# A fused retention and gated-convolution kernel: spreading the first batch over three engines, using spare PSUM banks for chunk 1, masks behind scores, value products between chunks

## Chip, cores, metric

One core of a Trainium2 chip (trn2). The metric is the device time of one execution in microseconds (us). A traced span is 1.7 to 2.2 us shorter than the time of the same run. The experiments ran on four chips, one for each group of kernels, together with the kernel before. Times of kernels in different groups are compared by their ratios to the kernel before, or by many runs together; single traces are also compared across groups. A run over 1.5% above the fastest of the same kernel counts as slow; ratios and means of "fast runs" leave it out.

## The reference

Retention (linear attention with a decay per head) feeds a gated unit: a causal depthwise convolution of five taps makes the gate, a matmul the value, their product goes through an output matmul.

```python
q, k, v: (8, 8, 576, 64) float32      # batch, heads, sequence, head size
scores = (q @ k.T) / sqrt(64)
ret    = scores * Dmat                # Dmat[i, j] = gamma_h ** (i - j) for i >= j, else 0
x      = (ret @ v) as (8, 576, 512)
gate   = sigmoid(sum_k conv_w[k] * x shifted by 4 - k)      # five taps
out    = (gate * (x @ w_val)) @ w_out                       # float32
```

## The kernel before

A sequence of 576 is cut into four chunks of 128 and a tail of 64, whose two halves of a pair of batches share a chunk: 36 chunks. A chunk runs these steps: keys turned on TensorE (`turn_k`), `scores`, `masks` on VectorE, the part from earlier chunks (`carried`), `values`, `take_x` (eviction with decay on VectorE), `update` of the state and `take_state` on ScalarE. Two chunks make a unit: `conv`, `gate` on ScalarE, two halves of `value` with a product z on VectorE, two halves of `project`. Engines run their own instruction streams in program order, so the order of the Python calls is the schedule. `keep_warm` issues matmuls whose result nobody reads. In this text DVE is VectorE, ACT ScalarE, POOL GpSimd, SP SyncE.

```python
ps_t  = ... bufs=1    # turned tiles "tps"          PSUM pools: 1 + 2 + 1 + 1 + 3 banks
ps_s  = ... bufs=1    # "s0", "s1": scores
ps_o  = ... bufs=1    # "o": output of a chunk
ps_st = ... bufs=1    # state
ps_g  = ... bufs=3    # "g": gates, values, projections, keep_warm

def load_keys(t):                     # float32 to bf16 during the transfer, GpSimd's queue
    kb = bfp.tile([P, H, D], BF16, name="kb", bufs=LA + 3)
    nc.gpsimd.dma_start(out=kb, in_=k[...])
def cast_k(t):                        # only chunk 0: loaded as float32 through SP's queue
    nc.vector.tensor_copy(kb, loaded["k", *chunks[t]])
def cast_v(t):
    nc.gpsimd.tensor_tensor(vb, loaded["v", ...], gin[...], op=ALU.mult)
def scores(t):
    s = [ps_s.tile([P, NP, P], F32, name=f"s{i}") for i in range(2)]
    ...
def carried(t):
    o = ps_o.tile([P, NP, P], F32, name="o")
    ...
# start of the program (cut: constants, diagonals, loads)
keep_warm(9)
for r in range(RQ):
    cast_q(("batch", 0, r), nc.vector if r % 2 else nc.gpsimd)
for r in range(RQ):
    turn_q(("batch", 0, r), s_copy if r % 2 else v_copy, ps_g if r < 3 else None)
cast_v(0); load_keys(2)
scores(0); turn_k(1); masks(0, 0); masks(0, 1); carried(0); update(0); take_state(0)
scores(1); values(0); cast_v(1); load_keys(3); take_x(0)
masks(1, 0); masks(1, 1); carried(1); update(1); take_state(1); values(1); take_x(1)
# ...
conv(0); gate(0, 0); gate(0, 1); load_wo()
turn_k(2); carried(2); scores(2); value(0, 0); masks(2, 0); cast_v(2); masks(2, 1); value(0, 1)
for t in sbl: nc.vector.memset(t, 0.0)
values(2); take_x(2); update(2); take_state(2)
turn_k(3); carried(3); scores(3); masks(3, 0); masks(3, 1); load_keys(4)
keep_warm(4); project(0, 0); project(0, 1); keep_warm(4)
cast_v(3); values(3); take_x(3); update(3); take_state(3); load_keys(5)
conv(1); gate(1, 0); gate(1, 1)
# ... cast_q of batch 1, cast_v(4), turn_k(4)
value(1, 0); turn_q(("batch", 1, 0)); value(1, 1)
# ... the other three turn_q, turn_k(5)
carried(4); update(4); scores(4); masks(4, 0); masks(4, 1)
for t in range(4, NT + 2):            # the loop; not touched but for where unit 1 starts
    ...
```

Of the kernel before, what the change touches and what calls it, by code (L numbers as in the profile page):

```python
# [21 lines left out]
def kernel(  # L22
# [48 lines left out]
    with tc.manual_schedule():  # L71
# [41 lines left out]
        load_one("k", k, *chunks[0], 1)  # L113
        load_queries(0)
        load(0)
# [40 lines left out]
        load_keys(1)  # L156
# [56 lines left out]
        def cast_k(t):  # L213
            kb = bfp.tile([P, H, D], BF16, name="kb", bufs=LA + 3)
            nc.vector.tensor_copy(kb, loaded["k", *chunks[t]])  # L215
            kbf[t] = kb

        def cast_v(t):
            vb = bfp.tile([P, H, D], BF16, name="vb")
            nc.gpsimd.tensor_tensor(vb, loaded["v", *chunks[t]],  # L220
                                    gin[:, chunks[t][2], :].unsqueeze(2).to_broadcast([P, H, D]), op=ALU.mult)
            vbf[t] = vb
# [4 lines left out]
        def cast_q(job, eng=nc.gpsimd):  # L227
            qb = bfp.tile([P, H, D], BF16, name="qb", bufs=5)
            if job[0] == "own":
                src = loaded["q", *chunks[job[1]]]  # L230
            else:
                src = loaded["qb", job[1]][:, :, job[2], :]
            eng.tensor_copy(qb, src)  # L233
            qbf[job] = qb
# [10 lines left out]
        def turn_k(t):  # L245
            ps = turned(kbf[t])
            kt = tp_sb.tile([P, NP, P], BF16, name="kt")
            nc.vector.tensor_copy(kt, ps)  # L248
            ktd[t] = kt

        def turn_q(job, copy=nc.scalar.copy, pool=None):
# [5 lines left out]
            else:  # L257
                b, r = job[1:]
                if r == 0:
# [12 lines left out]
        def scores(t):  # L272
            kt = ktd[t]
            s = [ps_s.tile([P, NP, P], F32, name=f"s{i}") for i in range(2)]
# [18 lines left out]
        def carried(t):  # L293

            kind, b, c = chunks[t]
            o = ps_o.tile([P, NP, P], F32, name="o")
# [142 lines left out]
        def keep_warm(n):  # L439

            idle = ps_g.tile([P, DM], F32, name="g")
# [5 lines left out]
        cast_k(0)  # L447
# [6 lines left out]
        keep_warm(9)  # L454
        for r in range(RQ):
            cast_q(("batch", 0, r), nc.vector if r % 2 else nc.gpsimd)
        for r in range(RQ):
            turn_q(("batch", 0, r), s_copy if r % 2 else v_copy, ps_g if r < 3 else None)
        cast_v(0)
        load_keys(2)  # L460
        scores(0)
        turn_k(1)
        masks(0, 0)
        masks(0, 1)
        carried(0)
        update(0)
        take_state(0)
        scores(1)
        values(0)
        cast_v(1)  # L470
        load_keys(3)
        take_x(0)
        masks(1, 0)
        masks(1, 1)
        carried(1)
        update(1)
        take_state(1)
        values(1)
        take_x(1)
        prep_wv(s_copy, 0)  # L480
        prep_wv(g_copy, 1)
# [3 lines left out]
        load_wo()  # L485
        turn_k(2)
        carried(2)
        scores(2)
        value(0, 0)
        masks(2, 0)  # L490
        cast_v(2)
        masks(2, 1)
        value(0, 1)
        for t in sbl:
            nc.vector.memset(t, 0.0)
# [4 lines left out]
        turn_k(3)  # L500
        carried(3)
        scores(3)
        masks(3, 0)
        masks(3, 1)
        load_keys(4)
        keep_warm(4)
        project(0, 0)
        project(0, 1)
        keep_warm(4)
        cast_v(3)  # L510
# [4 lines left out]
        load_keys(5)  # L515
# [3 lines left out]
        for r in range(RQ):  # L519
            cast_q(("batch", 1, r), nc.vector if r == 1 else nc.gpsimd)  # L520
        cast_v(4)
        turn_k(4)
        value(1, 0)
        turn_q(("batch", 1, 0))
        value(1, 1)
        load_keys(6)
        turn_q(("batch", 1, 1), v_copy, ps_g)
        turn_q(("batch", 1, 2), s_copy)
        turn_q(("batch", 1, 3), v_copy, ps_g)
        turn_k(5)  # L530
# [4 lines left out]
        masks(4, 1)  # L535
        load_keys(7)
        cast_v(5)

        for t in range(4, NT + 2):
# [36 lines left out]
            if unit and (odd or n > 1):  # L576
                part(n, 0)
            if jobs:
                turn_q(jobs[0])
            if unit and (odd or n > 1):  # L580
# [39 lines left out]
```

## Time and profile before

| | before |
|---|---|
| time, first three runs | 178.76 to 179.61 us, median 178.99 |
| the profiled run | time 177.88 us, span 176.1 us, mean granted TensorE clock 0.955 |
| conv(0), conv(1), conv(2) start | 18.40, 33.73, 49.73 us |
| conv(2) to the end | 126.4 us |
| TensorE busy, 70 to 170 us | 98.8 of 100 us |

The profile's rows and columns are explained where the prediction shows them. Two views matter most: the row PEclk (the clock that TensorE was granted, in tenths) and the chain that ended last, where each line is a piece of the path: start, length, engine, tile, line of code.

### The profile page before, as it was taken

What the parts mean: (1) busy time and instruction counts of PE and PEld (TensorE: products, weight loads), DVE (VectorE), ACT (ScalarE), POOL (GpSimd) and SP (SyncE); (2) the same over time, 40 slices, a digit from 0 to 9 for tenths busy, and PEclk for the clock granted to TensorE, in tenths of its full rate; (3) what the DMA queues carried; (4) which work ended last, traced back from release to release, by engine and by line L of the source; (5) the groups of instructions that cost most, each with busy time, mean ns of one, the idle gap of its engine ahead of it and who ended that gap; (6) DMA issues with size and microseconds to landing.
All of it is one profiled execution on the core that took longest, in us unless ns stands there. A gap on an engine that the chain in (4) does not pass through costs nothing.

```text
span 176.1 us, 5512 instructions
## 1 busy us (share of the span) xinstructions
PE 158.0 (90%) x2278; PEld 114.8 (65%) x2296; DVE 117.1 (66%) x225; ACT 87.3 (50%) x178; POOL 98.7 (56%) x129
## 2 busy tenths in 40 slices
PE   6775876887999999999999999999999999999970
PEld 1343654575586868677776868687776868677630
DVE  6556257477567677777767777877767688776330
ACT  6733401451375665656554665556575554545331
POOL 8598949466774666756685555757565534100000
PEclk9999589996599999999999999999999999999997
DMA  4999999999999999999989999999989994303114
GB/s 121 283 310 208 287 183 308 185 172 307 170 203 289 223 184 177 200 296 290 240 158 300 256 162 196 301 282 155 193 152 152 209 192 139 117 6 123 62 60 119
DMA packets 93958, 35.10 MB, mean 199 GB/s; under 512 B 80090, under 2 KB 88814, under 8 KB 93934
## 3 DMA queue, kind: packets, MB, share of 16 engines
q1 hardware_dynamic: 56704, 29.37, 63.4%
q0 software_dynamic: 37040, 5.11, 42.8%
q8 instruction: 18, 0.29, 0.7%
q10 hardware_dynamic: 190, 0.27, 0.6%
q14 instruction: 6, 0.05, 0.1%
HBM read 30.42 MB, written 9.44 MB: 226 GB/s over the span
## 4 chain that ended last, share of the span: by engine, by line
PE 76%; DVE 15%; issue 2%; ACT 2%; DMA 2%; ACTq 0%; DVEq 0%
PE g L398 18%; PE g L409 17%; PE g L383 13%; PE tps L240 9%; DVE p L287 7%; PE s L278 6%; PE o L319 5%; DVE z L401 5%; PE g L443 3%; PE st L350 2%; DVE xg L329 2%; DMA fkc<-in_k_dram 2%; PE o L302 2%; ACT qtb L262 1%; DVE kt L248 1%
## 5 line engine op out<-in xcount | busy, mean ns | idle before, releaser
L220 POOL TENSOR_TENSOR vb<-fvc,gin 128x512 bf16<-128x512 f32 x36 | 37.5, 1041 | 41.2 <-issue 17.9
L287 DVE TENSOR_TENSOR p<-s,maskq 128x512 bf16<-128x512 f32 x64 | 43.5, 686 | 16.4 <-PE s L278 16.1
L401 DVE TENSOR_TENSOR z<-gate,g 128x512 bf16<-128x512 f32 x36 | 24.8, 688 | 20.4 <-PE g L398 20.4
L398 PE MATMUL g<-xg,wvb 128*128 128x256 bf16 x288 | 37.4, 276 | 0.0
L412 ACT COPY ob<-g 128x512 f32<-128x512 f32 x36 | 21.1, 586 | 30.0 <-PE g L409 29.8
L409 PE MATMUL g<-wob,z 128*128 128x512 bf16 x127 | 33.8, 386 | 1.5 <-DVE z L401 0.5
L96 POOL DMA_DIRECT2D kb<-in_k_dram x31 | 29.4, 948 | 0.1
L391 ACT ACTIVATE gate<-g 128x512 f32<-128x512 f32 x36 | 19.5, 594 | 19.7 <-PE g L383 19.7
L398 PEld LDWEIGHTS <-wvb 128*128 128x128 bf16 x288 | 27.0, 99 | 3.5 <-issue 0.6
L361 ACT CAST sbd<-st 64x256 bf16<-64x256 f32 x48 | 17.6, 367 | 19.2 <-PE st L350 18.7
L383 PE MATMUL g<-xg,dg 64*64 64x256 bf16 x720 | 24.3, 279 | 1.2 <-DVE xg L329 1.2
L329 DVE TENSOR_TENSOR xg<-o,gout 128x512 bf16<-128x512 f32 x32 | 21.8, 681 | 4.2 <-PE o L319 4.2
L233 POOL CAST qb<-fqb 128x512 bf16<-128x512 f32 x29 | 18.0, 627 | 6.4 <-DMA fqb<-in_q_dram 5.0
L383 PEld LDWEIGHTS <-dg 64*64 64x64 bf16 x720 | 19.4, 109 | 3.3 <-issue 1.3
L409 PEld LDWEIGHTS <-z 128*128 128x128 bf16 x144 | 13.0, 100 | 11.2 <-DVE z L401 1.2
L248 DVE COPY kt<-tps 128x512 bf16<-128x512 bf16 x36 | 15.3, 424 | 6.2 <-PE tps L240 6.0
L262 ACT COPY qtb<-tps 128x512 bf16<-128x512 bf16 x27 | 15.9, 589 | 5.3 <-PE tps L240 5.3
L319 PE MATMUL o<-p,vb 128*64 128x128 bf16 x288 | 15.9, 232 | 1.3 <-DVE p L287 1.3
L278 PE MATMUL s<-qtb,kt 64*128 64x128 bf16 x256 | 13.8, 226 | 3.5 <-DVE p L287 2.4
L240 PE MATMUL tps<-ident,kb 128*128 128x128 bf16 x144 | 15.1, 231 | 1.3 <-DVE kb L215 0.8
L240 PEld LDWEIGHTS <-qb 128*128 128x128 bf16 x144 | 10.9, 100 | 4.5 <-issue 0.8
L278 PEld LDWEIGHTS <-kt 64*128 64x128 bf16 x288 | 8.9, 97 | 7.6 <-issue 1.8
(61 smaller groups left out, 139.7 us busy)
## 6 DMA issues: line engine op xcount, KB each, us to landing
fqb<-in_q_dram SPq DMA_DIRECT2D x8, 1024.0 KB, 8.0
fvc<-in_v_dram SPq DMA_DIRECT2D x32, 256.0 KB, 7.5
out_dram<-ob SPq DMA_DIRECT2D x32, 256.0 KB, 3.6
kb<-in_k_dram POOLq DMA_DIRECT2D x31, 128.0 KB, 6.8
wvf<-in_moe_w_val_dram SPq DMA_DIRECT2D x1, 1024.0 KB, 9.4
fqc<-in_q_dram SPq DMA_DIRECT2D x8, 128.0 KB, 5.4
fvc<-in_v_dram SPq DMA_DIRECT2D x8, 128.0 KB, 5.1
out_dram<-ob SPq DMA_DIRECT2D x6, 128.0 KB, 2.7
```

Source lines behind the costliest of these rows:

```text
L96: nc.gpsimd.dma_start(out=kb, in_=k[b, :, c * P:(c + 1) * P, :].rearrange("h p d -> p h d"))
L220: nc.gpsimd.tensor_tensor(vb, loaded["v", *chunks[t]], gin[:, chunks[t][2], :].unsqueeze(2).to_broadcast([P, H, D]), op=ALU.mult)
L240: nc.tensor.transpose(ps[:, pr, :], flat[:, pr * P:(pr + 1) * P], ident)
L278: nc.tensor.matmul(s[i][:, pr, :], lhsT=kt[r, pr, :], rhs=queries(t, r, pr), start=(pr == 0), stop=(pr == NP - 1), skip_group_check=True)
L287: nc.vector.tensor_tensor(p, sps[t][i], m.unsqueeze(1).to_broadcast([P, NP, P]), op=ALU.mult)
L319: nc.tensor.matmul(o[r, pr, :], lhsT=vb[:, 2 * pr + i, :], rhs=pt[t, i][:, pr, :], start=(fresh and pr == 0), stop=(pr == NP - 1), skip_gr ...
L329: nc.vector.tensor_tensor(by_token(x[:, bl, :, PAD + i0:PAD + i0 + P]), ops[t].rearrange("p o (r n) -> p o n r", r=RQ), by_token(gout[:, : ...
L383: nc.tensor.matmul(g[bank][cols, pr, :], lhsT=dg[rows, blk, kk, :], rhs=xs(n, rows, blk, kk), start=(pr == 0 and kk == 0), stop=(pr == 1 a ...
L398: nc.tensor.matmul(vps[:, j, :], lhsT=wvb[:, o, 2 * i + j, :], rhs=xs(n, slice(0, P), o, PAD), start=(j == 0 and o == 0), stop=(j == 1 and ...
L401: nc.vector.tensor_tensor(z, gsb[n][i], vps, op=ALU.mult)
L409: nc.tensor.matmul(o, lhsT=zsb[n, j // 2][:, j % 2, i * P:(i + 1) * P], rhs=wob[:, j, :], start=(j == 0), stop=(j == NP - 1))
L412: nc.scalar.copy(ob, o)
```

## The change

The intent is to start the loop earlier, with four things: the first batch's casts and turns on three engines (and chunk 1's keys loaded like chunk 0's); chunk 1's scores and output in banks of the pool of three; masks straight behind their scores, with eight `keep_warm` matmuls gone and five added elsewhere; unit 1's value products moved from in front of the loop to between chunks 4 and 5.

```diff
+        load_one("k", k, *chunks[1], 2)              # behind queries 0, SP's queue
-        load_keys(1)                                 # was at 2.66 us, GpSimd's queue
-        keep_warm(9)
-        for r in range(RQ):
-            cast_q(("batch", 0, r), nc.vector if r % 2 else nc.gpsimd)
-        for r in range(RQ):
-            turn_q(("batch", 0, r), s_copy if r % 2 else v_copy, ps_g if r < 3 else None)
-        cast_v(0)
+        keep_warm(7)
+        for (r, copy) in ((1, v_copy), (2, s_copy), (0, g_copy), (3, v_copy)):
+            cast_q(("batch", 0, r), copy)
         load_keys(2)
+        for (r, copy) in ((1, s_copy), (2, v_copy), (0, s_copy)):
+            turn_q(("batch", 0, r), copy, ps_g)
+        turn_q(("batch", 0, 3), v_copy)
+        cast_k(1, s_copy)
+        turn_k(1, s_copy)
+        cast_v(0, nc.vector)
         scores(0)
 ...
-        scores(1)
+        scores(1, spare=True)
+        masks(1, 0)
+        keep_warm(3, turn_bank=True)
         values(0)
 ...
+        carried(1, spare=True)
 ...
+        keep_warm(2, turn_bank=True)
         values(1)
         take_x(1)
+        turn_k(2)
+        carried(2)
+        scores(2)
+        masks(2, 0)
+        masks(2, 1)
         conv(0)
         gate(0, 0)
         gate(0, 1)
         value(0, 0)
         values(2)
 ...
-        turn_k(3)
+        turn_k(3, s_copy)
         carried(3)
         scores(3)
         masks(3, 0)
+        value(0, 1)
         masks(3, 1)
+        for t in sbl:
+            nc.gpsimd.memset(t, 0.0)
-        keep_warm(4)
         project(0, 0)
         project(0, 1)
-        keep_warm(4)
         values(3)
 ...                                                  # conv(1), gates, turns of batch 1 on DVE and ACT
         scores(4)
         masks(4, 0)
         masks(4, 1)
+        value(1, 0)                                  # value(1, 1) now runs in the loop's first round
+        turn_k(5)
```

More of the change, by code (lines that the diff above doesn't have):

```diff
@@ L112 @@
         nc.scalar.dma_start(out=cwn, in_=moe_conv_w.rearrange("k (o i) -> (k o) i", i=P))
-        load_one("k", k, *chunks[0], 1)
+        load_one("k", k, *chunks[0], 2)
         load_queries(0)
+        load_one("k", k, *chunks[1], 2)
         load(0)
@@ L210, in prep_wv, with cast_k, cast_v @@
                 copy(wvb[:, :, blk:blk + 2, j0:j0 + 64], src[:, :, :, ab, hl, :])
-        def cast_k(t):
+        def cast_k(t, copy):
             kb = bfp.tile([P, H, D], BF16, name="kb", bufs=LA + 3)
-            nc.vector.tensor_copy(kb, loaded["k", *chunks[t]])
+            copy(kb, loaded["k", *chunks[t]])
             kbf[t] = kb
-        def cast_v(t):
+        def cast_v(t, eng=nc.gpsimd):
             vb = bfp.tile([P, H, D], BF16, name="vb")
-            nc.gpsimd.tensor_tensor(vb, loaded["v", *chunks[t]],
+            eng.tensor_tensor(vb, loaded["v", *chunks[t]],
                                     gin[:, chunks[t][2], :].unsqueeze(2).to_broadcast([P, H, D]), op=ALU.mult)
@@ L225, with cast_q @@
         qbf, qtd = {}, {}
-        def cast_q(job, eng=nc.gpsimd):
+        def cast_q(job, copy=nc.gpsimd.tensor_copy):
             qb = bfp.tile([P, H, D], BF16, name="qb", bufs=5)
@@ L232, in cast_q @@
                 src = loaded["qb", job[1]][:, :, job[2], :]
-            eng.tensor_copy(qb, src)
+            copy(qb, src)
             qbf[job] = qb
@@ L243, with turn_k @@
         ktd = {}
-        def turn_k(t):
+        def turn_k(t, copy=nc.vector.tensor_copy):
             ps = turned(kbf[t])
             kt = tp_sb.tile([P, NP, P], BF16, name="kt")
-            nc.vector.tensor_copy(kt, ps)
+            copy(kt, ps)
             ktd[t] = kt
@@ L258, in turn_q @@
                 b, r = job[1:]
-                if r == 0:
+                if ("batch", b) not in qtd:
                     qtd["batch", b] = tp_sb.tile([P, NP, RQ, P], BF16, name="qtb", bufs=2)
@@ L270, with scores @@
         sps = {}
-        def scores(t):
+        def scores(t, spare=False):
             kt = ktd[t]
-            s = [ps_s.tile([P, NP, P], F32, name=f"s{i}") for i in range(2)]
+            s = [ps_g.tile([P, NP, P], F32, name="g") if spare else ps_s.tile([P, NP, P], F32, name=f"s{i}")
+                 for i in range(2)]
             for pr in range(NP):
@@ L291, with carried @@
         state = {}
-        def carried(t):
+        def carried(t, spare=False):
             kind, b, c = chunks[t]
-            o = ps_o.tile([P, NP, P], F32, name="o")
+            o = ps_g.tile([P, NP, P], F32, name="g") if spare else ps_o.tile([P, NP, P], F32, name="o")
             ops[t] = o
@@ L437, with keep_warm @@
         rhs0 = sbd[0].rearrange("p o j -> p (o j)")
-        def keep_warm(n):
-            idle = ps_g.tile([P, DM], F32, name="g")
+        def keep_warm(n, turn_bank=False):
+            idle = ps_t.tile([P, DM], F32, name="tps") if turn_bank else ps_g.tile([P, DM], F32, name="g")
             for _ in range(n):
@@ L446 @@
         keep_warm(6)
-        cast_k(0)
+        cast_k(0, v_copy)
         turn_k(0)
@@ L453 @@
         prep_diagonals(3, nc.gpsimd)
-        keep_warm(9)
-        for r in range(RQ):
-            cast_q(("batch", 0, r), nc.vector if r % 2 else nc.gpsimd)
-        for r in range(RQ):
-            turn_q(("batch", 0, r), s_copy if r % 2 else v_copy, ps_g if r < 3 else None)
-        cast_v(0)
-        load_keys(2)
+        keep_warm(7)
+        for (r, copy) in ((1, v_copy), (2, s_copy), (0, g_copy), (3, v_copy)):
+            cast_q(("batch", 0, r), copy)
+        load_keys(2)
+        for (r, copy) in ((1, s_copy), (2, v_copy), (0, s_copy)):
[4 more added lines that the diff above has]
+        cast_v(0, nc.vector)
         scores(0)
-        turn_k(1)
         masks(0, 0)
         masks(0, 1)
+        cast_v(1)
+        load_keys(3)
+        load_wo()
         carried(0)
@@ L467 @@
         take_state(0)
-        scores(1)
+        scores(1, spare=True)
+        masks(1, 0)
+        keep_warm(3, turn_bank=True)
         values(0)
-        cast_v(1)
-        load_keys(3)
         take_x(0)
-        masks(1, 0)
         masks(1, 1)
-        carried(1)
+        carried(1, spare=True)
         update(1)
         take_state(1)
+        prep_wv(s_copy, 0)
+        prep_wv(g_copy, 1)
+        cast_v(2)
+        load_keys(4)
+        keep_warm(2, turn_bank=True)
         values(1)
         take_x(1)
-        prep_wv(s_copy, 0)
-        prep_wv(g_copy, 1)
+        turn_k(2)
[3 more added lines that the diff above has]
+        masks(2, 1)
         conv(0)
@@ L484 @@
         gate(0, 1)
-        load_wo()
-        turn_k(2)
-        carried(2)
-        scores(2)
         value(0, 0)
-        masks(2, 0)
-        cast_v(2)
-        masks(2, 1)
-        value(0, 1)
-        for t in sbl:
-            nc.vector.memset(t, 0.0)
+        cast_v(3)
+        load_keys(5)
         values(2)
@@ L503 @@
         masks(3, 0)
+        value(0, 1)
         masks(3, 1)
-        load_keys(4)
-        keep_warm(4)
+        for t in sbl:
+            nc.gpsimd.memset(t, 0.0)
         project(0, 0)
         project(0, 1)
-        keep_warm(4)
-        cast_v(3)
         values(3)
@@ L514 @@
         take_state(3)
-        load_keys(5)
+        turn_k(4, s_copy)
+        for (r, copy) in ((0, g_copy), (1, v_copy), (2, g_copy), (3, s_copy)):
+            cast_q(("batch", 1, r), copy)
+        cast_v(4)
+        load_keys(6)
         conv(1)
@@ L518 @@
         gate(1, 1)
-        for r in range(RQ):
-            cast_q(("batch", 1, r), nc.vector if r == 1 else nc.gpsimd)
-        cast_v(4)
-        turn_k(4)
-        value(1, 0)
-        turn_q(("batch", 1, 0))
-        value(1, 1)
-        load_keys(6)
-        turn_q(("batch", 1, 1), v_copy, ps_g)
-        turn_q(("batch", 1, 2), s_copy)
-        turn_q(("batch", 1, 3), v_copy, ps_g)
-        turn_k(5)
+        turn_q(("batch", 1, 1), v_copy)
+        turn_q(("batch", 1, 3), s_copy, ps_g)
+        turn_q(("batch", 1, 0), v_copy)
+        turn_q(("batch", 1, 2), s_copy, ps_g)
         carried(4)
@@ L575 @@
             part = project if odd else value
-            if unit and (odd or n > 1):
+            if unit and t > 4:
                 part(n, 0)
@@ L579 @@
                 turn_q(jobs[0])
-            if unit and (odd or n > 1):
+            if unit:
                 part(n, 1)
```

## The prediction

> **What bounds the kernel now.** I read the page's 40 slices first, then a table of busy time in chosen stretches, then the chain that ended last in order of time, then the timeline of the first 66 us, and last the landing times of single transfers. In the slices the two rows that carry it are TensorE's busy share and its granted clock:
>
> ```profile
> PE   6775876887999999999999999999999999999970
> PEclk9999589996599999999999999999999999999997
> ```
>
> A slice is 4.4 us. From the eleventh slice on TensorE is full; the first ten, 44 us, are between 5 and 8 tenths, and the clock falls to half twice (slice 5; slices 10 and 11). The stretches say the same (busy us of PE, PEld, DVE, ACT, POOL, then clock, DMA share, GB/s):
>
> ```profile
> 10.00:20.00 10.00, 5.99 (x97) 4.98 (x99) 5.05 (x9) 3.68 (x8) 9.44 (x13) 0.84 1.33 284
> 20.00:30.00 10.00, 7.49 (x80) 5.13 (x74) 5.79 (x13) 1.82 (x4) 7.40 (x10) 0.82 1.40 243
> 40.00:50.00 10.00, 9.00 (x99) 6.02 (x103) 5.79 (x11) 3.29 (x8) 6.73 (x11) 0.66 1.29 231
> 70.00:170.00 100.00, 98.83 (x1561) 74.25 (x1573) 73.85 (x127) 54.53 (x114) 48.59 (x58) 1.00 1.00 187
> ```
>
> From 70 to 170 us TensorE is busy 98.8 of 100 us: that part is bound by its work, the diff leaves its loop body alone, and it can only be moved earlier or later. So the whole question is when the loop gets under way. As the marker I take the start of conv(2), the first thing in the loop that has the same neighbours before and after the change. The chain, in order of time (start, us, what), cut to what fixes that marker:
>
> ```profile
> 11.79 0.40 PE s L278 x8
> ...
> 12.99 1.21 DVE p L287 x2
> 14.19 0.05 issue
> 14.24 0.40 PE s L278 x7
> 14.63 0.36 PE o L319 x8
> ...
> 18.40 2.35 PE g L383 x36
> ...
> 33.73 1.29 PE g L383 x40
> ...
> 39.05 0.38 PE s L278 x8
> ...
> 49.80 1.22 PE g L383 x40
> ```
>
> Scores(0) at 11.79, then scores(1) only at 14.24, behind both masks of chunk 0, since both use the two score banks; conv(0) at 18.40, taking 2.35 us where conv(1) takes 1.29 (half clock); scores(4) at 39.05; conv(2) at 49.80. The chain up to there hops between TensorE, masks (0.61 to 0.69 us each on DVE), evictions and turned copies: a latency chain, not one engine's load.
>
> **What the Trainium skill says.** "TensorE: Matmul & The Clock Gate", Part 1, says the clock is either half or full, decided on a free-running window of about 3.4 us by how busy TensorE was. The trace agrees: the one-microsecond table gives clock 0.93 at 16 to 17, 0.66 at 23 to 24, 0.87 at 40 to 41 and 0.71 at 47 to 48, which put the changes at 16.86, 23.68, 40.74 and 47.6, each a multiple of 3.41 apart. The half-clock stretches here last 6.8 us. "PSUM — Partial Sum Buffer", Specifications, gives eight banks a partition; the kernel's pools take 1+2+1+1+3 = 8, so "spare banks" are the three of the gate pool, idle between the query turns and conv(0). "SBUF — State Buffer", Who interferes with whom, says VectorE and GpSimd share ports while ScalarE waits for nobody; in this trace a query cast on DVE takes 0.43 us alone and 1.17 beside a GpSimd product, and one on GpSimd 0.61 alone and 0.81 beside DVE. "DMA: Bandwidth & Descriptors", Issuing engines are not separate DMA queues, says all issuers share the same engines; so moving the second key chunk from GpSimd's queue to SP's saves no bytes, only changes its place: here it was issued at 2.66 us and landed 8.8 us later, at 11.5.
>
> **The change, part by part**, walked forward with the durations of this trace (turn of four transposes 0.22, its copy from PSUM 0.42 on DVE and 0.59 on ACT and starting 0.41 after the turn; scores 0.33, first mask 0.43 after they start; mask 0.61; values 0.35, take_x 0.69; conv 1.22; half of value 0.87; half of project 0.86; hops 0.04).
>
> *First batch over three engines.* Queries land at 8.6. Casts went two and two on DVE and GpSimd and ended at 10.26; now ACT takes one, and they end by 9.8. Warming drops from 9 matmuls to 7 (0.43 each at half clock), so TensorE is free at 9.25, not 10.1. All four turned queries are ready at about 11.2 instead of 11.75. But the key cast and turn of chunk 1 now stand on ACT and TensorE ahead of scores(0), which start at 12.0, a little later than 11.79. The copy of chunk 1's keys no longer stands on DVE between scores and masks (0.42 us), so masks(0) begin at 12.5, not 13.0.
>
> *Second chunk in spare banks.* Scores(1) need no mask of chunk 0: 12.85 instead of 14.24. DVE now runs mask, mask, mask back to back to 14.3, take_x(0) to 15.1, the last mask to 15.7; values(1) at 15.75 instead of 17.04, take_x(1) ends at 16.9 instead of 18.36. **Gain so far 1.4 us.** Five warming matmuls (0.22 each) fill waits for masks and cost nothing.
>
> *Masks behind scores, unit products between chunks.* Key chunk 2 is issued at about 9.3 and, at the 6.6 to 7.1 us of its neighbours, lands at 16.4, just in time. Scores(2) 17.4, conv(0) 17.75 at full clock (1.22, not 2.35), value(0,0) 19.0, values(2) 19.85, scores(3) 22.0, value(0,1) behind them to 23.2, project(0) ends 25.45 (it waits for the second z until 24.1), values(3) 25.8, take_x(3) 26.65 instead of 33.69. Eight warming matmuls (1.9 us on the chain), four clears of sbl on DVE (1.1 us, 0.82 of it on the chain) and about 2.5 us of half clock have gone. **Gain 7 us.** Keys 4 (issued at 19, landing near 27.3 at 8.3 us) then hold turn_k(4) and with it conv(1), 27.5 instead of 33.73: gain 6.2.
>
> *Second batch.* Cast and turned over DVE and ACT under conv(1): the last copy waits for both gates and another copy on ACT and ends at 31.25; scores(4) 31.3 instead of 39.05. Value(1) is no longer done before that but is woven into chunks 4 and 5, so 1.74 us of TensorE work moves behind the marker scores(4); it lies beside masks of chunk 4 (31.7 to 32.95), z and copy of keys 5, so it costs little. Scores(5) 34.1, scores(6) 37.6, then values(5), project(1), four turns and scores(7) in TensorE's own time, 4.2 us: conv(2) at 41.8 instead of 49.80. **Sum: 8.0 us** if the clock stays full and no transfer is late.
>
> **Rivals.** (1) The clock falls in the new gap. From 30.5 to 33.9 I count scores, half of value, a turn and an update, 1.6 us in a window of 3.4; before, a window with about 1.9 us (37.3 to 40.7, mostly transposes) led to half clock and one with 2.0 (27.1 to 30.5) did not. I give it two chances in three. It would last 6.8 us as both did before; the first half is DVE's chain, where it costs some 0.8 us, the second is TensorE's, about 1.5: 2.3 us, so 1.5 on average. (2) A transfer takes the place of the removed waits. GpSimd waited 2.19 us for values 4, landed 26.1, and the queue moves 240 to 280 GB/s in this stretch whatever TensorE does; queries 2 landed at 31.9, values 6 at 33.3, keys 6 would now land near 35, when turn_k(6) is wanted at 35.6. All are met with less than a microsecond or a few; I take 0.8 us off. If the inputs were the real bound the gain would shrink to 3 or 4 us and the time be near 175.5. Against it: before, values 5 were cast at 29.2 but used at 44, so there is reserve. (3) GpSimd, with the weights' casts, the outputs' weight loads and now the clears, becomes the pace: 9.4 of 10 us busy from 10 to 20. It loses a key load, a query cast and a product to others, and would be at values(2)'s product by 18.3, wanted at 19.85: close, but not binding. (4) Nothing is gained, since TensorE is 90% busy: refuted by the ten slices in front, where about 8 us were waits or half clock.
>
> **Range and chances.** 8.0 less 1.5 for the clock less 0.8 for transfers leaves 5.7: 178.99 - 5.7 = 173.3 us. With everything in time and the clock full it is 171.0; with half clock twice and transfers late, near 176.4. Two per cent is 3.6 us, so faster needs below 175.4, which leaves 2.1 us for error: 0.80. Within 2% 0.18. Slower would need a hold-up of over 9 us against my walk: 0.02.
>
> **What would show it.** Right: conv(2) starts near 43 to 44, conv(0) takes 1.2 to 1.3 us before 18.5, scores(1) start before the masks of chunk 0 end, scores(4) are near 31.5, and from conv(2) to the end the same 126 us pass. Step wrong: if conv(0) takes over 2 us, the fillers failed to hold the clock; if conv(1) or scores(4) come after 34 with GpSimd or SP waiting on transfers, rival 2; if the loop is longer than 126 us, the reserve of prefetch has been eaten and shows as DMA waits later. The prediction fails most likely by the clock: its window is free-running, so one fall more or less is worth 2 us either way.

## The result

| first measurement, one chip | before | change |
|---|---|---|
| runs | 178.08, 178.76, 178.99, 179.61 | 170.41, 170.67, 173.06, 173.52 |
| median | 178.88 | 171.87 |
| ratio of fast runs | | 0.9542 (0.9488 to 0.9596) |

A ratio is the mean time of one kernel's fast runs over that of the other's in the same rounds, so it isn't quite the ratio of the medians. The change is faster by 4.6%. The forecast was 173.3 us, 171.0 to 176.4; the ratio times 178.88 is 170.7 us, just below that range, while the median of all four runs is inside it. (A fifth run of the change took 170.91.) The change's runs came in two groups, and the profile (span 171.1 us, time 173.06) fell in the slower one. A faster run was profiled later (span 169.2 us); both are shown.

The slices of the change, slower run:

```profile
PE   6876588777999999999999999999999999999970
PEclk9999879999999999999999999999999999999998
```

The front is still uneven, but the loss of clock is one short stretch in slices 5 and 6, and the one at 40 us is gone. The same by stretches:

```profile
10.00:20.00 10.00, 5.54 (x79) 3.25 (x81) 5.72 (x10) 4.49 (x10) 7.93 (x12) 1.00 1.31 235
20.00:30.00 10.00, 8.47 (x100) 5.47 (x102) 4.56 (x7) 3.28 (x7) 5.28 (x9) 0.83 1.29 238
...
40.00:50.00 10.00, 9.34 (x152) 7.14 (x153) 6.50 (x12) 5.85 (x13) 5.83 (x10) 1.00 1.24 253
...
70.00:165.00 95.00, 93.88 (x1478) 70.75 (x1484) 69.65 (x121) 51.47 (x107) 47.07 (x57) 1.00 1.01 192
```

From 10 to 20 us TensorE is busy 5.54 us, less than before (5.99): the front was not made denser. The loop is as full as before. The chain of the slower run, cut to the marks:

```profile
8.54 0.81 POOL qb L233
9.35 9.26 DMA kb<-in_k_dram
...
18.66 0.41 PE tps L240 x4
...
19.57 0.40 PE s L279 x8
19.97 2.27 PE g L384 x40
22.24 1.54 PE g L399 x8
...
34.30 0.40 PE s L279 x8
...
44.90 1.22 PE g L384 x40
```

The second line is the surprise: 9.26 us of the chain are the transfer of chunk 2's keys, on which turn_k(2) waits. Then conv(0) and value(0, 0) run on half clock (2.27 and 1.54 us, against 1.22 and 0.98 at full). The faster run, same view:

```profile
9.24 9.12 DMA kb<-in_k_dram
...
18.40 0.41 PE tps L240 x4
...
19.32 0.40 PE s L279 x8
19.72 1.22 PE g L384 x40
...
32.44 0.40 PE s L279 x8
```

Keys 2 are as late, but conv(0) has the full clock: that, not the keys, makes most of the difference between these two traces. (The mean clock is 0.987 in both, with one fall of 3.4 us each; it is where the fall lies that differs.) Whether it also made the two groups is not shown. In the timelines:

| start, us | before | walk of the prediction | change, slower run | change, faster run |
|---|---|---|---|---|
| conv(0) | 18.40 | 17.75 | 19.90 | 19.65 |
| conv(1) | 33.73 | 27.5 | 30.80 | 28.93 |
| scores(4) | 38.98 | 31.3 | 34.30 | 32.44 |
| conv(2) | 49.73 | 41.8 | 44.83 | 42.96 |
| conv(2) to end | 126.4 | 126 | 126.3 | 126.3 |

The loop from conv(2) on takes the same time in all; the whole gain is in front of it. And conv(0) starts later than before: all of the gain lies between conv(0) and conv(2), where before took 31.3 us and the change takes 23.3 (24.9 in the slower run).

### The profile page after: what moved, and what is told of

Its sections match the earlier page's. It is cut to its first block, busy times and chain, and to the rows that moved or that the text cites. A ratio compares the mean times of both kernels' runs of the same rounds, so it can differ in the third digit from the quotient of the medians.

```text
span 171.1 us, 5513 instructions
## 1 busy us (share of the span) xinstructions
PE 153.4 (90%) x2272; PEld 111.0 (65%) x2291; DVE 114.2 (67%) x219; ACT 90.3 (53%) x184; POOL 96.9 (57%) x129
## 4 chain that ended last, share of the span: by engine, by line
PE 70%; DVE 10%; DMA 10%; ACT 4%; issue 2%; POOL 0%; ACTq 0%; SPq 0%; DVEq 0%
PE g L399 19%; PE g L410 16%; PE g L384 13%; PE tps L240 8%; DMA kb<-in_k_dram 5%; PE s L279 5%; PE o L320 5%; DVE p L288 5%; DVE z L402 5%; DMA fqb<-in_q_dram 4%; PE st L351 3%; PE o L303 1%; ACT qtb L262 1%; DVE kt L248 1%; ACT ob L413 1%
## 5 line engine op out<-in xcount | busy, mean ns | idle before, releaser
L288 DVE TENSOR_TENSOR p<-s,maskq 128x512 bf16<-128x512 f32 x62 | 42.3, 686 | 17.8 <-PE s L279 17.6
L220 POOL TENSOR_TENSOR vb<-fvc,gin 128x512 bf16<-128x512 f32 x35 | 36.4, 1041 | 29.1 <-issue 12.4
L410 PE MATMUL g<-wob,z 128*128 128x512 bf16 x126 | 32.9, 379 | 2.0 <-DVE z L402 1.1
L96 POOL DMA_DIRECT2D kb<-in_k_dram x30 | 28.2, 942 | 0.1
L233 POOL CAST qb<-fqb 128x512 bf16<-128x512 f32 x27 | 16.4, 615 | 12.7 <-DMA fqb<-in_q_dram 12.7
L240 PE MATMUL tps<-ident,kb 128*128 128x128 bf16 x144 | 14.5, 224 | 3.8 <-DMA kb<-in_k_dram 2.4
L262 ACT COPY qtb<-tps 128x512 bf16<-128x512 bf16 x24 | 14.1, 589 | 4.2 <-PE tps L240 4.2
L248 DVE COPY kt<-tps 128x512 bf16<-128x512 bf16 x33 | 14.0, 424 | 2.9 <-PE tps L240 2.8
L279 PE MATMUL s<-qtb,kt 64*128 64x128 bf16 x248 | 12.3, 219 | 3.3 <-DVE kt L248 2.3
L320 PE MATMUL o<-p,vb 128*64 128x128 bf16 x280 | 14.5, 225 | 0.0
L240 PEld LDWEIGHTS <-kb 128*128 128x128 bf16 x144 | 8.5, 98 | 9.2 <-issue 2.8
```

Source lines behind the costliest of these rows:

```text
L96: nc.gpsimd.dma_start(out=kb, in_=k[b, :, c * P:(c + 1) * P, :].rearrange("h p d -> p h d"))
L220: eng.tensor_tensor(vb, loaded["v", *chunks[t]], gin[:, chunks[t][2], :].unsqueeze(2).to_broadcast([P, H, D]), op=ALU.mult)
L240: nc.tensor.transpose(ps[:, pr, :], flat[:, pr * P:(pr + 1) * P], ident)
L279: nc.tensor.matmul(s[i][:, pr, :], lhsT=kt[r, pr, :], rhs=queries(t, r, pr), start=(pr == 0), stop=(pr == NP - 1), skip_group_check=True)
L288: nc.vector.tensor_tensor(p, sps[t][i], m.unsqueeze(1).to_broadcast([P, NP, P]), op=ALU.mult)
L320: nc.tensor.matmul(o[r, pr, :], lhsT=vb[:, 2 * pr + i, :], rhs=pt[t, i][:, pr, :], start=(fresh and pr == 0), stop=(pr == NP - 1), skip_gr ...
```

## The experiments

Sixteen experiments ran in four groups, each group on one chip; three of them are the change itself again. All gave the right result. The kernel before ran 11 times in each group, 44 in all. A ratio below is to the kernel before of the same group; its 95% interval is 0.5 to 1.1% either way, so it tells no smaller differences apart.

### The change again: after_again

> The changed kernel unchanged, to see its faster runs in a profile. The profile on record (span 171.1 us) is of a slow run: turn_k(2) waited 2.39 us for keys 2, which landed 9.3 us after issue, TensorE then fell to half clock from 20.0 to 23.4, and conv(2) began at 44.9. Theory A (data): in a fast run (span 168.4 to 168.9) keys 2 land 2 us or so earlier, turn_k(2) starts by 16.9, the half-clock stretch of 3.4 us is gone or falls on little work, and conv(2) begins near 42.3. Theory B (clock): keys 2 land near 18.6 in the fast run as well and the half-clock stretch lies elsewhere. Either way from conv(2) to the end 126.2 us, and times in two groups, near 170.6 and 173.3.

Measured: 171.04 to 172.72 us, median 171.48; before 175.28 to 179.69; ratio 0.9705 (0.964 to 0.977). Theory B is right for the chain: keys 2 landed 9.1 us after issue in the faster profile too, and the half-clock stretch (3.4 us, from 11.1 to 14.5) lay on the scores of chunks 0 and 1 and on warming matmuls, in front of the wait for keys 2, which hid it. The two sharp groups expected did not return; times were spread over 1.7 us.

The larger lesson was in the kernel before. Its 44 runs sort by granted clock (correlation of clock and time -0.93):

| granted clock of before | runs | us |
|---|---|---|
| 0.978 to 0.979 | 13 | 175.3 to 175.8 |
| 0.950 to 0.965 | 21 | 176.6 to 178.3 |
| 0.937 to 0.947 | 10 | 178.3 to 179.7 |

Going from 0.978 to 0.955 adds some 8 us of half clock and 2.4 us of time. The four runs of the first measurement, 178.08 to 179.61, all fit the two slower groups; the profiled one had 0.955. The 18 runs of the change in three later groups have clocks of 0.972 to 0.997 and 170.35 to 172.77 us. Set against the 13 runs of before with the highest clock (mean 175.55), they are still 3.8 us faster on average (171.74, at a mean clock of 0.987): most of the gain is not that the change avoids before's slower clock states.

### Keys 2 earlier, first try: early_k2

```diff
+        load_keys(2)                                 # where load_keys(1) stood before, 2.66 us
         mask_q = consts.tile(...)
 ...
-        load_keys(2)
```

> One line moved: GpSimd issues the load of keys 2 before it makes the query mask, at 2.7 us as keys 1 were in the kernel before, not behind its query cast at 9.35. Theory A (data): keys 2 land near 12, turn_k(2) follows values(1) at 16.3, TensorE has no idle 2.4 us at 16 to 18.6, conv(0) starts near 17.7 at full clock, conv(2) near 41.8 as the walk had it; time 170.0 or less in every run, with no group at 173. Theory B (the wait is absorbed by queries 1, landing at 27.0, and values 4 at 29.6): conv(0) earlier, but conv(2) and the time as in the faster runs of the change, 170.6.

Measured: 170.82 to 172.16, median 171.24, ratio 0.9687 against 0.9705 beside it: nothing gained that can be told. The wait for keys 2 had gone, but conv(0) began at 19.26. The load had pushed the query mask's copy on GpSimd to 3.75 us, beside VectorE's cast of the first keys:

```profile
3.75 0.76 POOL L161 COPY maskq<-mask 128x128 bf16<-128x128 bf16 x1
```

```profile
4.00 0.80 DVE L217 CAST kb<-fkc 128x512 bf16<-128x512 f32 x1 [0.27 <-DMA fkc<-in_k_dram]
```

The two fences are the timelines of GpSimd and VectorE in this run. The cast takes 0.80 us where in the change it takes 0.43. The Trainium skill, "SBUF — State Buffer", Who interferes with whom, says casts can take a port pair that GpSimd shares and that one then blocks the other; that agrees. The first turn came 0.44 us later, and in this run the clock came up only at 15.3, so many of the steps in front of conv(0) ran at half clock. (The run's mean clock of 1.000 doesn't show it, and the stretches from 8 to 15 us give 1.00 as well: the mean leaves out what lies in front of the first recorded change. The durations show it: four transposes took 0.61 us instead of 0.40.) The trial said nothing clear on keys 2 and was repeated below.

### Without the five fillers: no_fillers

```diff
-        keep_warm(3, turn_bank=True)
-        keep_warm(2, turn_bank=True)
```

> The change without the 3 and 2 warming matmuls between scores(1) and values(1). My walk called them free. If they hold the clock as intended, without them the clock falls to half at about 17 us for 6.8 us, conv(0) takes 2.3 us and scores and value(0) twice as long: 2 to 4 us slower than the change in fast runs. If they don't matter (the clock fell at 20.0 with them as well, because of the wait for keys 2), the time is within 1 us of the change.

Measured: 170.84 to 173.06, median 171.48, the same median as the change (0.9707 and 0.9705). In its profile the clock fell at 15.2 for 6.8 us and conv(0) took 2.35 us, as the first theory said; yet the loss in time was not to be seen. It had reached turn_k(2) 1.3 us sooner in that run, since its queries and keys 2 had landed sooner. From conv(0) to the end it took 151.2 us, 1.6 more than after_again. So the trace shows a cost of the missing fillers that the times of four runs don't; what the fillers are worth stays open.

### Chunk 1 in its own banks: own_banks

```diff
-        scores(1, spare=True)
+        scores(1)
-        carried(1, spare=True)
+        carried(1)
```

> The change with scores(1) and carried(1) in their old banks. The walk: scores(1) then wait for both masks of chunk 0, at 13.5 not 12.4, and their masks come 1.1 to 1.4 us later; values(1) at 17 not 15.3. If keys 2 hold turn_k(2) until 18.6 anyway, that delay is hidden and the time is within 0.5 us of the change; if keys 2 come earlier in fast runs, the loss is 1 to 1.4 us.

Measured: 170.75 to 171.46 and one slow run of 173.70, median 171.26, ratio 0.9674 (0.959 to 0.976): no difference from the change that can be told. Turn_k(2) started at 17.90 and conv(0) at 19.41. The later scores(1) (its main part at 13.19, against 12.48) vanished in the wait for keys 2, which landed at 17.9.

### The kernel before with its gaps filled: before_warm

```diff
         scores(1)
+        keep_warm(3)
         values(0)
 ...
+        keep_warm(3)
         values(1)
 ...
+        keep_warm(3)
         carried(4)
         update(4)
         scores(4)
+        keep_warm(4)
```

> The kernel before, with warming matmuls in its idle gaps and nothing else: three ahead of values(0), three ahead of values(1), three ahead of carried(4) and four behind scores(4). It takes the clock falls out of the kernel before, if low TensorE activity makes them. In eleven runs on the last chip the kernel before had times from 175.3 (granted clock 0.978) to 179.7 (0.946), while the change had 171.0 to 172.7 at 0.985 to 0.992. Theory C (much of the measured gain, and of the spread, is the clock): granted clock 0.98 or better in nearly all runs, times near 174 to 175.5 with no group at 178 to 180; the change's remaining lead over it is then about 3 to 4 us of shorter waits. Theory D (the clock's falls lie on waits and cost little): the times stay spread from 175 to 180, or all rise by the added matmuls, up to 2 us.

Measured: 177.41 to 178.66, ratio 1.0068: not faster. The spread shrank to 1.25 us from the 4 us of before, as theory C has it, but the mean did not fall. In the profile the second fall had gone (clock full from 20.8 on), and conv(1) to conv(2) took 14.85 us instead of 16.0. The first had not: it came at 14.0, and the fillers themselves then ran at half clock in the chain:

```profile
15.11 1.39 PE g L443 x3
16.50 0.59 PE o L319 x8
...
18.94 1.28 PE g L443 x3
20.22 0.59 PE o L319 x8
...
21.58 1.29 PE g L383 x40
```

In the chain's view of this run, above, three warming matmuls cost 1.39 us, where at full clock (0.22 each) they would take some 0.65, and conv(0) started at 21.58 instead of 18.40. Filling the gaps is no substitute for the change.

### The first batch's part undone: first_undone

```diff
 # from the change: keys 1 again through load_keys(1), keep_warm(9), casts and turns on two engines, cast_v(0) on GpSimd
+        cast_v(0)
+        load_keys(2)
         scores(0)
+        turn_k(1)
```

> The change with its first-batch part undone: nine warming matmuls, query casts and turns on two engines, keys 1 on GpSimd's queue early, product of values 0 on GpSimd, keys 2 issued at 11.2 us; the spare banks and all that follows stay. The walk gave this part 0.5 to 0.6 us up to take_x(1). But keys 2 hold turn_k(2) (18.4 in the change), and undone they are issued 1.9 us later: if they land 8 to 9 us after that, at 19.5 to 20, the loss is 1 to 2 us and is the load's place, not the three engines. If they land by 18 as in the kernel before (6.6 us), the time is within 0.5 us of the change: the part as such is hidden.

Measured: 170.49 to 171.94, ratio 0.9704, like the change in three other groups (0.9705, 0.9741, 0.9704). Keys 2 were issued at 11.0, 1.8 us later, and turn_k(2) still started at 17.67, earlier than in the change: they landed after 6.6 us. The part as such is hidden.

### Unit 1's value products ahead of the loop: unit_front

```diff
         gate(1, 1)
+        value(1, 0)
         turn_q(("batch", 1, 1), v_copy)
+        value(1, 1)
 ...
-        value(1, 0)
         turn_k(5)
```

> The change with both half value products of unit 1 back ahead of the loop, between the gates and the query turns, as in the kernel before. In the change scores(4) are at 32.4, and from there to conv(2) 10.5 us pass. Walk: 1.74 us of TensorE work goes in front of scores(4), of which some lies beside the gates on ScalarE and the turned copies (0.5 to 1 us), and chunks 4 and 5 then have waits that nothing fills: scores(4) about 1 us later, and of chunks 4 and 5 about as long as before since VectorE's chain sets them: 0.7 to 1.5 us slower than the change. Rival: without that work TensorE is idle from 33 to 37 and the clock falls there, as it did at 40.7 in the kernel before: 2 to 3 us slower, with granted clock 0.96 or below.

Measured: 173.30 to 174.22, ratio 0.9822, clocks 0.962 to 0.980, where fill_back on the same chip had 0.9668 and 0.983 to 0.992. Both theories hold together. Conv(1) to scores(4) took 5.1 us instead of 3.5, and the gap after it was left empty:

```profile
36.00:37.00 1.00, 0.00 (x0) 0.00 (x0) 1.00 (x3) 0.00 (x0) 1.00 (x3) 1.00 1.65 197
37.00:38.00 1.00, 0.92 (x20) 0.73 (x21) 0.51 (x2) 0.00 (x0) 0.98 (x2) 1.00 1.14 132
38.00:39.00 1.00, 0.30 (x6) 0.18 (x4) 1.00 (x3) 0.00 (x0) 1.00 (x2) 1.00 1.09 154
39.00:40.00 1.00, 0.89 (x14) 0.62 (x14) 0.73 (x2) 0.29 (x1) 1.00 (x3) 0.55 1.51 251
40.00:41.00 1.00, 1.00 (x18) 0.63 (x15) 0.57 (x1) 0.44 (x2) 0.84 (x3) 0.50 1.48 317
```

(Columns as before; TensorE's busy time is the first after the length, the clock the third from the end.) TensorE has nothing from 36 to 37 and little from 38 to 39, and the clock falls at 39.1 for 3.4 us. So, as far as one profile and the clocks of four runs show, the moved products also keep the clock: the fall that I had given two chances in three, in this gap around scores(4), came in none of the four profiles of the change.

### The removed fillers and clears put back: fill_back

```diff
         for t in sbl:
-            nc.gpsimd.memset(t, 0.0)
+            nc.vector.memset(t, 0.0)
+        keep_warm(4)
         project(0, 0)
         project(0, 1)
+        keep_warm(4)
```

> The change with the eight warming matmuls about project(0) and the four clears on VectorE put back, as in the kernel before. I had called their removal a gain of 1.9 and 0.8 us on the chain. In the changed kernel the first four would lie in the wait for the second z (0.64 us of 0.86) and the clears in an idle 1.3 us of VectorE, so: values(3) 1.0 to 1.2 us later and the time 1.0 to 1.3 us longer, not 2.7; if the chain through ScalarE from the project copies on hides that too, under 0.5.

Measured: 170.30 to 171.69, ratio 0.9668: no loss to be seen in time. In the profile conv(0) to conv(1) took 10.43 us instead of 9.28, so 1.15 us, as expected; but that run had its queries 0.6 us earlier and reached conv(0) at 18.05. By the trace, what the change removed here is worth about 1.1 us, not the 2.7 of my walk; by the times, nothing that can be told.

### Halves of the change: after_c, second_only, first_only

second_only is the kernel before up to take_x(1) and then the change; first_only the reverse, with the loop's start as before.

> The changed kernel again, as the measure for the three beside it on the same chip. By the traces so far conv(0) starts near 19.5, set by turn_k(2) and keys 2 (17.7 to 18.6), and from there to the end 149.5 us pass with the clock full, 151.2 where conv(0) and value(0,0) fall on half clock. Time 170.5 to 172.7.

> Only the second half of the change: up to take_x(1) the kernel before (two engines, keys 1 through GpSimd, chunk 1 in its own banks, no fillers there), then the change (masks behind scores, unit products between chunks). Theory E (the first half is swallowed by the wait for keys 2): conv(0) starts at 19.2 to 19.7 as in the change, 149.5 us follow, and the time is within 0.6 us of the change run beside it. Theory F (the walk: the first half is worth 1.4 us to the end): 1.2 to 2 us slower than the change. If the clock falls before conv(0), as in the kernel before at 16.86, it adds 1.6 us to either.

> Only the first half of the change: up to take_x(1) the change, then the kernel before (conv(0) straight after, masks interleaved, warming matmuls round project, unit 1's value products ahead of the loop). Conv(0) does not wait for keys 2 here and can start at 17.0, 1.4 us before the kernel before. Theory E: keys 2 and 3 then hold scores(2), and from conv(2) on all is as before: at most 0.5 us better than the fast runs of before, 175 or more. Theory F: 1.4 us better at equal clock; where the fillers keep the clock through conv(0), the fast runs are near 173.5.

| same chip | us | mean of fast runs | ratio to before |
|---|---|---|---|
| before | 175.47 to 179.64 | 176.64 | 1 |
| after_c (the change) | 171.56 to 172.77 | 172.22 | 0.9741 |
| second_only | 171.56 to 173.15 | 172.68 | 0.9765 |
| first_only | 173.41 to 177.43 | 174.45 | 0.9867 |

The second half alone gives nearly the whole gain: second_only is 0.5 us behind the change, and its profile has conv(0) at 19.42, theory E. The first half alone isn't worthless without the second: first_only is 2.2 us better than before. Some of that is clock (0.972 to 0.990 in its fast runs): set against runs of before with 0.978 (175.5), its runs with 0.982 (174.0 and 174.2) are 1.4 us better, near theory F's number (some 0.4 of it may be the slightly higher clock: across the 44 runs of before, 0.023 of clock went with 2.4 us). So the first half is worth 1.0 to 1.4 us by itself, and loses most of it when put in front of the second half, where conv(0) stands behind turn_k(2) and so behind keys 2. after_c also showed the other side of the clock: its fall came at 18.65, on conv(0) (2.15 us), and from conv(0) to the end its profile took 150.5 us, after_again's, with the fall at 11.1, 149.6, and the change's slower run, with the whole fall on conv(0) and value(0, 0), 151.2.

### Keys 2 settled: after_d, k2_behind_mask, k2_late

```diff
 # k2_behind_mask
         nc.gpsimd.tensor_copy(mask_q...)
+        load_keys(2)                                 # issued at 3.1 us
 # k2_late: load_keys(2) behind cast_v(1), issued at 12.5 us
```

> The changed kernel as the measure on the same chip: keys 2 issued at 9.3 us, turn_k(2) at 18.4 to 18.7, conv(0) at 19.6 to 20.3, time 171 to 172.7.

> Keys 2 issued early again, but behind the query mask (at 3.5 us, GpSimd idle until 5.8), not ahead of it: the earlier trial had pushed the mask's copy beside VectorE's cast of the first keys, which took 0.72 instead of 0.43 us, so TensorE began 0.45 us later and the clock came up late, at 15.3. If the wait for keys 2 is what the walk missed, TensorE reaches turn_k(2) at 16.3 to 16.6, conv(0) at 17.7 to 18.2, and the time is 1.2 to 1.9 us below the change. If early keys 2 only delay queries 0 and values 0 and 1 by as much, conv(0) stays at 19 or later and the gain is under 0.5 us.

> The suspected wait made longer: keys 2 issued behind the product of values 1, at 12.6 instead of 9.3 us. If keys 2 set conv(0) and all after it moves rigidly, with keys landing 7 to 9 us after issue (19.6 to 21.6) the time rises by 1 to 3 us over the change, conv(0) by the same. If their landing is set by what the queues carry and not by the issue (before: issued 11.2, landed 17.8), conv(0) and time move by less than 0.5 us.

| same chip | us | mean of fast runs | ratio to before | keys 2 issued, turn_k(2) starts | conv(0) |
|---|---|---|---|---|---|
| after_d (the change) | 170.35 to 172.74 | 171.36 | 0.9704 | 9.66, 18.63 | 19.87 |
| k2_behind_mask | 169.28 to 170.64 | 170.08 | 0.9632 | 3.12, 15.84 | 17.35 |
| k2_late | 170.72 to 174.22 | 172.09 | 0.9746 | 12.53, 20.23 | 21.90 |

The TensorE timeline of k2_behind_mask, turned keys, scores and convs alone:

```profile
15.84 0.40 PE L241 MATMUL tps<-ident,kb 128*128 128x128 bf16 x4
17.02 0.40 PE L280 MATMUL s<-qtb,kt 64*128 64x128 bf16 x8 [0.56 <-DVE kt L249]
17.35 1.29 PE L385 MATMUL g<-xg,dg 64*64 64x256 bf16 x40
...
27.41 0.40 PE L241 MATMUL tps<-ident,kb 128*128 128x128 bf16 x4 [0.26 <-DMA kb<-in_k_dram]
27.74 1.29 PE L385 MATMUL g<-xg,dg 64*64 64x256 bf16 x40
31.18 0.40 PE L280 MATMUL s<-qtb,kt 64*128 64x128 bf16 x8 [0.47 <-ACT qtb L263]
...
41.71 1.29 PE L385 MATMUL g<-xg,dg 64*64 64x256 bf16 x40
```

and the first line of the same view of the change's faster run (after_again), for comparison:

```profile
18.40 0.40 PE L240 MATMUL tps<-ident,kb 128*128 128x128 bf16 x4 [1.46 <-DMA kb<-in_k_dram]
```

With the keys in time, turn_k(2) follows values(1) without a wait, conv(0) starts 2.5 us earlier than in after_d, and the time falls by 1.3 us; five of after_d's six runs are slower than all six of this kernel. It isn't the clock alone: after_d's profile had a fall of 3.4 us in front of turn_k(2) and this one none, but the four runs of k2_behind_mask with a clock of 0.993 or more average 169.9 us and the three of after_d with 0.992 or more 171.1. The other 1.1 us go into the next wait of the kind: turn_k(4) now waits for keys 4 (issued at 18.45, landed 8.9 us later) and holds conv(1), as the walk had said of it. From there the trace is the prediction's walk to within 0.3 us: conv(1) 27.74 (walk 27.5), scores(4) 31.18 (31.3), conv(2) 41.71 (41.8), span 168.1, which is 176.1 less 8.0. k2_late issues keys 2 some 3 us later than after_d; turn_k(2) came 1.6 us later in its profile (a slow run), and its fast runs lost 0.7 us, which the spread of these runs doesn't tell from nothing. The wait is real, and the landing depends only in part on the issue. Why the change's keys 2 take about 9 us is not shown: the kernels that load keys 1 through GpSimd's queue issued keys 2 at 11.0 to 11.2 us and had them after 5.6 to 6.6. The change also put the 256 KB of keys 1 onto SP's queue; no run separates that from the time of issue.

### A version that beats both: tuned, tuned2

The change with keys 2 early (tuned as in early_k2, tuned2 behind the mask), and:

```diff
-        values(2) ... turn_k(3, s_copy); carried(3); scores(3); masks(3, 0); value(0, 1); masks(3, 1)
+        turn_k(3, s_copy); values(2) ... scores(3); masks(3, 0); value(0, 1); masks(3, 1); carried(3)
+        load_keys(6); load_keys(7)                   # ahead of the casts and of cast_v(4)
-        (1, v_copy), (2, g_copy), (3, s_copy)        # cast_q of batch 1
+        (1, v_copy), (2, g_copy), (3, v_copy)
-        conv(1); gate(1, 0); gate(1, 1); turn_q x4 (two on ScalarE)
+        conv(1); turn_q(1); turn_q(0, s_copy); gate(1, 0); gate(1, 1); turn_q(2, ps_o); turn_q(3, ps_s)
-        value(1, 0); turn_k(5)
+        turn_k(5, s_copy); value(1, 0)               # and turn_k(6, s_copy)
```

> An attempt to beat both, from the waits that the change's trace leaves: keys 2 issued at 2.7 us; turn_k(3) ahead of values(2), so scores(3) don't wait for ScalarE's state and key copies (1.1 us); keys 6 and 7 issued ahead of the wait for values 4; the fourth query cast on VectorE and the turned queries copied ahead of the gates, three of four on VectorE (0.4 us); turned keys 5 and 6 copied by ScalarE, so scores(5) and scores(6) don't stand behind VectorE's z (1 us). Expected: scores(3) at 22.6 not 24.1, scores(4) near 31, conv(2) near 40.5 not 42.9, and 168.5 to 169.5 us. If queries 1 (24 to 27 us) and values 4 (26 to 29) hold it instead, scores(4) stay at 32 and the gain is under 1 us.

> The tuned kernel (169.84 us beside the change's 172.25) with keys 2 issued behind the query mask as well. Conv(0) at 17.7 to 18.2 instead of 19.15 and 1 us off: 168.5 to 169.3 us. If queries 1 or values 4 and 5 now hold scores(4), it stays at 169.5 to 170.

tuned: 168.90 to 172.21 (one slow run), ratio 0.9595, beside 0.9741 of the change. tuned2: 168.97 to 174.38 (one slow run), ratio 0.9599, beside 0.9704 of the change; its median, 169.31 us, is the lowest of all. Its conv(2) starts at 40.06, but from there to the end 127.1 us pass, 0.8 more: the loop's first rounds now wait for inputs, as rival 2 had it. TensorE's and GpSimd's timelines in tuned2:

```profile
37.52 0.40 PE L242 MATMUL tps<-ident,qb 128*128 128x128 bf16 x4 [1.21 <-POOL qb L234]
...
46.03 0.40 PE L242 MATMUL tps<-ident,kb 128*128 128x128 bf16 x4 [0.74 <-DMA kb<-in_k_dram]
```

```profile
35.87 1.03 POOL L221 TENSOR_TENSOR vb<-fvc,gin 128x512 bf16<-128x512 f32 x1 [4.47 <-DMA fvc<-in_v_dram]
```

GpSimd stood 4.47 us waiting for values 6, so the query casts behind them came late and TensorE waited 1.21 us for one; later it waited 0.74 us for keys. Starting the loop still earlier will need the inputs sooner.

## Why the prediction was right or wrong

**Right: what bounds and where.** The loop is TensorE's and fixed; conv(2) to the end took 126.3 us in all four profiles of the change. The direction, the mechanism (waits and half clock in front of the loop) and rival 4's refusal held.

**Right: the sum of the walk.** 8.0 us from the profiled run of before (span 176.1) was reached to a tenth of a microsecond, not by the change but by k2_behind_mask (168.1).

**Wrong: keys 2 "land at 16.4, just in time".** I took 6.6 to 7.1 us from issue to landing, from neighbours issued at other times, though keys 1 in the same trace took 8.8; it was 8.9 to 9.3 in the change's four profiles. That step of the walk is off by 2 us, and with it conv(0): 19.65 instead of 17.75. The allowance for transfers, 0.8 us, was too small: putting the keys in time gave 1.3 us of measured time. The 1.4 us of "first batch" and "spare banks" ended in this wait: own_banks and first_undone each cost nothing that can be told.

**Wrong: the clock falls from 30.5 to 33.9, "two chances in three", 1.5 us.** It fell there in no profile of the change. The products moved between chunks seem to hold it: unit_front, which takes them away, has a fall of 3.4 us at 39.1 in its one profile. The change does have one fall of 3.4 us in each of its four profiles, but earlier: on conv(0) and value(0, 0) it cost 0.9 to 1.6 us from there to the end, in front of the wait for keys 2 it was hidden. Busy TensorE time, which I used to judge, was the wrong measure (see the last section).

**Wrong: the base, and with it the range's low end.** I wrote that 171.0 is what remains "with everything in time and the clock full", which is 178.99 less 8.0. But the 8.0 had been walked in the trace of a run that took 177.88 us. From that run, 8.0 less is 169.9, and the forecast would have been 172.2: this one step put forecast and range 1.1 us too high. From 173.3 down to the 170.7 measured are 2.6 us. This step is 1.1 of them. About 0.9 is the half clock that didn't come, less the keys that came late: the change's faster profile belongs to a run of 171.25 us, 6.6 below 177.88 where 5.7 was forecast. Some 0.6 stays open. (The last two are differences of times; no run measures them apart.)

Nor is the base one number: the kernel before has 175.3 to 179.7 by its clock, and the first measurement drew four from the upper end, while two of the change's four were among its best. Over 44 runs of before and 18 of the change in later groups the means are 177.37 and 171.74 (not all on the same chips, slow runs counted): 5.6 us, against the 5.7 that I had forecast. That agreement is in part luck, since two wrong terms (clock too large, transfers too small) partly offset each other.

**Mis-sized within the walk:** eight warming matmuls and the clears were put at 2.7 us; put back they cost 1.15 in the trace and nothing clear in the times. Behind the second z and in VectorE's idle time the rest was free already.

**Open:** why the fast runs of the change in the first measurement (170.4 to 170.9) lie below all of those in two of the three later groups (from 171.04 and 171.56 up); none of them was profiled.

## What to carry to other kernels

A step that is made faster in front of a transfer that lands later still gives nothing: look for the landing of each input that stands on the path, one by one, at the load of that moment, before summing gains of compute. Work placed in a gap of TensorE can be worth more than its own time, since it also keeps the clock; plain fillers gave no such gain here. Where the base has states, give a forecast for each of them, or the range is too narrow, and subtract a gain from the run in whose trace it was read.

## What the Trainium skill lacked or had wrong

- "TensorE: Matmul & The Clock Gate", Part 1, puts the return to half clock at a window that was idle; its part on a second failure mode tells of short idles between groups of matmuls that make the clock swing, without saying how many it takes. Here it came after windows in which TensorE was busy for half the time: 1.78 of 3.42 us (13.44 to 16.86, kernel before) and 1.94 of 3.41 (no_fillers, 11.83 to 15.24).
- The same page has no measure of activity that tells which windows lead to a fall. Busy time doesn't: the change kept the full clock after a window with 1.79 us (33.61 to 37.03, of which 0.39 transposes), as little as those that fell.
- The same page puts the ramp at the start at under 1% of a typical span, and for falls within a kernel it has one case, matmuls that wait for data 32 times (53.3 of 211 us at half clock). A kernel with one or two falls isn't on it: in this kernel one and the same program took 175.3 to 179.7 us, 2.5% apart, nearly in order of its granted clock.
- "DMA: Bandwidth & Descriptors", Latency and other measured facts, gives first-byte times near 1 us and an HBM latency of up to 2 us at high load. No page has the time to landing of a transfer behind others: the 128 KB of chunk 2's keys took 5.6 to 10.1 us over the profiled runs here, while the queues moved 235 to 284 GB/s (10 to 30 us, before and change).
